# An mLSTM-and-bilinear kernel: a block's result copies move to the tiles in which weights were put together

## The chip, the cores and the metric

The kernel runs on one core of a Trainium2 chip. The metric is the time of one execution on the device in microseconds (us). Five engines work side by side, each through its own list of instructions in a fixed order: TensorE (PE; its weight loads are shown as PEld), VectorE (DVE), ScalarE (ACT), GpSimd (POOL), and SyncE (SP), which here only issues DMAs. An instruction that waits holds up all that stand behind it on its engine.

## The reference

Two stages follow each other. The first is an mLSTM attention over 4 batches, 8 heads, 768 steps and a head size of 40: a gated recurrence with a matrix state per head,

```
m_new = max(f + m, i);  F = exp(f + m - m_new);  I = exp(i - m_new)
C = F * C + I * v k^T;  n = F * n + I * k
y = sigmoid(o) * (C q) / max(|n.q|, 1)
```

The second takes y as 3072 tokens of 320 values and computes a bilinear feed-forward layer of width 1536:

```
a = x @ w_a;  b = x @ w_b;  out = (a * b) @ w_out
```

The three weight matrices arrive as 64-bit floats.

## The kernel before, in words

**Attention.** The tokens are cut into 24 chunks of 128 (6 time steps of a chunk for each of 4 batches). A chunk goes through a row of stages: its q and k are split into bf16 pieces and transposed by DMA, scores are made on PE (`pS`, line 468), weighted with exponentials of gate sums (ACT, line 413) and split again on DVE and ACT (lines 473 to 479, `pb`), multiplied with v (`pV`, line 520), joined with the state's share (`num`), divided and gated (`den`, `osig`, lines 591 to 613), and transposed on PE into x (`pX`, line 630). Output gates for four chunks are loaded and put through a sigmoid at once (`load_o`, line 169).

**Feed-forward.** Chunks form 9 blocks of 2 or 3 chunks: 2, 2, 3, 3, 3, 3, 3, 2, 3. `moe_block(kb)` walks through the width in 12 pieces of 128, `ff` = 0 to 11. `up(ff)` makes two products `acc[0]` and `acc[1]` of eight matmuls each (line 743) in PSUM, in three buffers that go round (tag `pu`). Line 750 copies `acc[0]` into a tile `g` in SBUF; DVE does it for ff = 1 and 2, ACT for all others. Line 751 (DVE) multiplies `acc[1]` into `g`. Lines 753 and 755 split `g` into `gh` and `gl`. `down(ff)` (line 716) follows two pieces later and adds to one PSUM tile `pd` for each chunk of the block. After ff = 11 each `pd` is copied by ACT to a tile `o` (line 725), and SP issues its DMA to `out` (line 726).

**Buffers.** `g` and `o` share a tag, `acp`, with three buffers of 384 fp32 values in each partition; a buffer comes free when the last reader of its tile is done, which for an `o` is its DMA. The tag `cv` has four buffers of the same size. They hold `cw`, in which a stage of the weights is put together from the halves of its 64-bit words (lines 342 to 375). The trace has the last instruction that touches a `cw` (line 373) at 92.3 us.

**Order.** While block kb runs through the feed-forward, the attention of a later block's chunks is handed out in between (`run_block`). For blocks 2 to 8 the order on PE and on SP is as the code is written; on ACT, DVE and POOL a planner sets it from its own estimate of when each instruction can start. SP takes its list in order: behind a block's last attention product it loads gate sums (`gbc`, line 180) and states (`cx`, line 587), and then come the `o` DMAs.

## Time and profile before

| | |
|---|---|
| median of 3 runs | 588.99 us (588.3 to 591.35) |
| the profiled execution, its own time | 591.32 us |
| its span, first to last instruction | 589.5 us |
| PE busy | 546.1 us (93%) |
| PEld busy | 516.2 us (88%) |
| DVE busy | 408.6 us (69%) |
| ACT busy | 221.8 us (38%) |
| POOL busy | 125.0 us (21%) |
| mean granted clock of TensorE | 0.948 |

A timeline row reads: start and length in us, engine, line, operation, what it writes and reads, how many were merged, and in brackets how long its engine stood idle before it and what ended that. A row of a view of waits reads: who waited for whom, us in total, how often, the longest. A row of the view by stretches gives, after the stretch and its length, the busy time of PE, PEld, DVE, ACT and POOL, each with its count of instructions, then the granted TensorE clock, the share of the DMA engines that was busy and GB/s.

### The profile page before, as it was taken

How to read it: one execution, taken by the hardware profiler on the slowest of the kernel's cores; microseconds unless marked ns; L12 is line 12 of the kernel's file. 1: busy time of each engine (PE TensorE's matmuls, PEld its weight loads, DVE VectorE, ACT ScalarE, POOL GpSimd, SP SyncE). 2: the span in 40 equal slices, each digit the busy share in tenths (PEclk: the TensorE clock that was granted, in tenths of full speed). 3: DMA queues.
4: the chain of work that ended last, by engine and by line, in shares of the span. 5: the costliest groups of instructions: out<-in, count | busy, mean ns of one | idle time of the engine just before them, and what ended most of it. 6: DMA issues, size and time to landing. Idle time of an engine off the chain costs nothing.

```text
span 589.5 us, 12444 instructions
## 1 busy us (share of the span) xinstructions
PE 546.1 (93%) x4810; PEld 516.2 (88%) x4810; DVE 408.6 (69%) x967; ACT 221.8 (38%) x530; POOL 125.0 (21%) x185
## 2 busy tenths in 40 slices
PE   9586899998999998999989998999969997899997
PEld 6485899987999987999879997999969997889997
DVE  6899676459978774878677893877649575744432
ACT  5677754434433451333431341542322324211011
POOL 2011245343332213033032132033020102000000
PEclk9687589989999999999989999899979999999999
DMA  9999513668838856358656665767543942300000
GB/s 182 277 271 271 104 37 83 130 102 146 163 92 167 145 99 131 70 113 174 102 122 132 102 123 129 101 134 154 79 110 40 166 75 71 73 1 24 0 1 34
DMA packets 198679, 66.77 MB, mean 113 GB/s; under 512 B 184252, under 2 KB 191900, under 8 KB 198620
## 3 DMA queue, kind: packets, MB, share of 16 engines
q1 hardware_dynamic: 198620, 65.98, 55.2%
q8 instruction: 38, 0.62, 0.5%
q14 instruction: 21, 0.17, 0.1%
HBM read 41.11 MB, written 5.97 MB: 80 GB/s over the span
## 4 chain that ended last, share of the span: by engine, by line
PE 69%; DMA 7%; DVE 4%; ACT 3%; issue 3%; SPq 2%; POOL 1%; POOLq 0%; ACTq 0%; DVEq 0%
PE pu L743 39%; PE pd L716 18%; PE pV L520 3%; DMA out_dram<-o 3%; PE pS L468 2%; PE pU L544 1%; DMA osig<-in_o_gate_dram 1%; PE pX L630 1%; SPq L587 1%; PE pI L494 1%; PE pS L817 1%; DMA T<-qks 1%; PE pV L869 1%; ACT gbc L413 1%; SPq L160 1%
## 5 line engine op out<-in xcount | busy, mean ns | idle before, releaser
L743 PE MATMUL pu<-xh,w 128*128 128x384 f32 (+1 forms) x1080 | 288.4, 334 | 20.6 <-ACT g L750 17.5
L743 PEld LDWEIGHTS pu<-xh,w 128*128 128x128 f32 x1080 | 198.6, 197 | 25.2 <-ACT g L750 19.4
L743 PE MATMUL pu<-xl,w 128*128 128x384 f32 (+1 forms) x648 | 214.2, 333 | 1.0 <-DVE xl L636 1.0
L716 PE MATMUL pd<-w,gh 128*128 128x320 f32 x576 | 133.4, 316 | 1.0 <-ACT gh L753 1.0
L743 PEld LDWEIGHTS pu<-xl,w 128*128 128x128 f32 x648 | 127.5, 197 | 2.0 <-DVE xl L636 1.3
L716 PEld LDWEIGHTS pd<-w,gh 128*128 128x128 f32 x576 | 98.4, 191 | 1.7 <-ACT gh L753 1.2
L751 DVE TENSOR_TENSOR g<-pu,g 128x384 f32<-128x384 f32 (+1 forms) x108 | 54.8, 507 | 58.7 <-PE pu L743 56.0
L750 ACT COPY g<-pu 128x384 f32<-128x384 f32 (+1 forms) x92 | 40.5, 441 | 139.6 <-PE pu L743 116.5
L716 PE MATMUL pd<-w,gl 128*128 128x320 f32 x288 | 89.9, 318 | 0.0
L455 POOL TENSOR_TENSOR vr<-va 128x336 f32<-128x336 f32 x18 | 13.6, 753 | 203.2 <-PE pV L520 188.0
L716 PEld LDWEIGHTS pd<-w,gl 128*128 128x128 f32 x288 | 54.3, 191 | 0.1
L413 ACT ACTIVATE gbc<-gbc,gtab 128x128 f32<-128x128 f32 x160 | 49.2, 390 | 11.6 <-POOL gbc L406 11.5
L755 DVE TENSOR_TENSOR gl<-g,gh 128x384 fp32r<-128x384 f32 (+1 forms) x92 | 50.3, 548 | 1.6
L527 DVE TENSOR_TENSOR num<-pV,num 128x336 f32<-128x336 f32 x18 | 9.1, 506 | 38.9 <-PE pV L520 38.8
L753 DVE CAST gh<-g 128x384 fp32r<-128x384 f32 (+1 forms) x96 | 34.0, 355 | 1.6
L475 ACT CAST pb<-gbc 128x512 bf16<-128x512 f32 x36 | 22.2, 617 | 20.4 <-DVE gbc L473 20.2
L562 ACT CAST cb<-cst 128x168 bf16<-128x168 f32 x18 | 6.0, 332 | 62.4 <-DMA gbc<-g_dram 40.8
L473 DVE TENSOR_TENSOR gbc<-pS,gbc 128x512 f32<-128x512 f32 x36 | 24.6, 683 | 5.2 <-PE pS L468 5.1
L406 POOL TENSOR_SCALAR_AFFINE_SELECT gbc<-gbc 128x1024 f32<-128x1024 f32 x20 | 23.4, 1168 | 21.6 <-DMA gbc<-g_dram 19.0
L520 PEld LDWEIGHTS <-pb 128*128 128x128 bf16 x576 | 23.1, 96 | 4.2 <-DVE pb L479 1.8
L520 PE MATMUL pV<-va,pb 128*128 128x42 bf16 x288 | 25.1, 182 | 1.6 <-DVE pb L479 1.6
L607 POOL TENSOR_TENSOR osig<-osig,den 128x320 f32<-128x320 f32 x22 | 16.9, 766 | 43.8 <-DVE den L602 25.4
(130 smaller groups left out, 804.0 us busy)
## 6 DMA issues: line engine op xcount, KB each, us to landing
gbc<-g_dram SPq DMA_DIRECT2D x20, 512.0 KB
qk<-in_q_dram SPq DMA_DIRECT2D x24, 160.0 KB
qk<-in_k_dram SPq DMA_DIRECT2D x24, 160.0 KB
va<-in_v_dram SPq DMA_DIRECT2D x24, 160.0 KB
osig<-in_o_gate_dram SPq DMA_DIRECT2D x24, 160.0 KB
raw<-in_moe_w_out_dram SPq DMA_DIRECT2D x12, 320.0 KB
out_dram<-o SPq DMA_DIRECT2D x24, 160.0 KB
raw<-in_moe_w_a_dram SPq DMA_DIRECT2D x8, 384.0 KB
```

The lines of the kernel that those rows point to most:

```text
L406: nc.gpsimd.affine_select(E, E, pattern=[[0, H], [1, P]], compare_op=ALU.is_ge, fill=-1e30, base=0, channel_multiplier=-1,)
L413: nc.scalar.activation(E[:, h], E[:, h], AF.Exp, bias=beta[:, h:h + 1])
L473: nc.vector.tensor_tensor(E, pS, E, op=ALU.mult)
L475: nc.scalar.copy(pb[:, 0], E)
L520: nc.tensor.matmul(pv[:, h], pb[i][:, h % HH, :], vb[j][:, h], start=(x == 0), stop=(x == len(terms) - 1),)
L607: (nc.vector if n < NS else nc.gpsimd).tensor_tensor(yv, yv, den.unsqueeze(2).broadcast_to([P, H, D]), op=ALU.mult)
L716: nc.tensor.matmul(pd[t][:, 0:DM], a[:, cols], w, start=(ff == 0 and first), stop=(ff == NF - 1 and last),)
L743: up_in = nc.tensor.matmul(acc[j], a, r, start=(x == 0), stop=(x == len(terms) - 1),).ins
L750: (nc.vector.tensor_copy if kb > 0 and ff in [1, 2] else nc.scalar.copy)(g, acc[0])
L751: nc.vector.tensor_tensor(g, acc[1], g, op=ALU.mult)
L753: (nc.vector.tensor_copy if kb > 0 else nc.scalar.copy)(gh, g)
L755: (nc.gpsimd if kb * 12 + ff < 16 else nc.vector).tensor_tensor(gl, g, gh.bitcast(F32), op=ALU.subtract)
```

## The change

Result tiles `o` of blocks 1 to 8 are taken from the four `cv` buffers instead of the three `acp` buffers. Block 0, during which weights are still put together, keeps `acp`. Sizes, instructions and DMAs are the same; no pool grows.

```diff
             if ff == NF - 1:
                 for t in range(sizes[kb]):
                     c, b = chunks[begins[kb] + t]
-                    o = mpool.tile([P, NTB], F32, tag="acp", name=f"o{kb}_{t}")[:, 0:DM]
+                    pool, tag, bufs = (cpool, "cv", CVB) if kb > 0 else (mpool, "acp", 3)
+                    o = pool.tile([P, WCH], F32, tag=tag, name=f"o{kb}_{t}", bufs=bufs)[:, 0:DM]
                     nc.scalar.copy(o, pd[t][:, 0:DM])
                     nc.sync.dma_start(out[b * S + c * P:b * S + (c + 1) * P, :], o)
```

The diff adds one line, so all below line 724 stands one line further down in the changed kernel (750 becomes 751). The orders of PE, SP and POOL are the same in both kernels. On ACT and DVE the planner places instructions differently around the ends of blocks. At the end of block 2 and the start of block 3 ACT's list reads, before (semaphores that an instruction waits for are in brackets; those of DMAs begin with DMAHW):

```order
L725 COPY o_0_3131<-pd_0_2187 128x320 [waits PE_49]
L725 COPY o_1_3134<-pd_1_2188 128x320 [waits DVE_49,PE_49]
L725 COPY o_2_3137<-pd_2_2189 128x320 [waits DVE_49,PE_49]
L562 CAST cb_3262<-cst_95 128x168 [waits DMAHW1_49,DMAHW0_49,DMAHW6_49,DVE_49,DMAHW7_49,Activation_49,Pool_49]
L750 COPY g_0_3157<-pu_0_0_3143 128x384 [waits DMAHW1_49,PE_49,Activation_49]
```

and in the changed kernel:

```order
L726 COPY o_0_3131<-pd_0_2187 128x320 [waits PE_49]
L726 COPY o_1_3134<-pd_1_2188 128x320 [waits PE_49]
L726 COPY o_2_3137<-pd_2_2189 128x320 [waits PE_49]
L751 COPY g_0_3157<-pu_0_0_3143 128x384 [waits DVE_49,PE_49]
L562 CAST cb_3262<-cst_95 128x168 [waits DMAHW1_49,DMAHW0_49,DMAHW6_49,DVE_49,DMAHW7_49,Activation_49,Pool_49]
```

The first copy of the next block's `g` no longer waits for a DMA, and it stands ahead of a state's cast (`cb`). The starts of blocks 4, 5, 6 and 7 lose the same wait.

On DVE, from the same place on, before:

```order
L527 TENSOR_TENSOR num_3018<-pV_3167,num_3018 128x336
L600 SCALAR_TENSOR_TENSOR den_3234<-num_3018 128x8
L601 TENSOR_SCALAR den_3234<-den_3234 128x8
L602 RECIPROCAL den_3234<-den_3234 128x8
L555 TENSOR_TENSOR cst_95<-pU_3241,cst_95 128x168
L610 TENSOR_TENSOR osig_2498<-num_3018,osig_2498 128x320
L435 TENSOR_TENSOR r_0_3307<-qk_80,qks_89 128x320
L612 COPY osig_2498<-osig_2498 128x64
L436 CAST qks_89<-r_0_3307 128x8x40
L750 COPY g_1_3253<-pu_1_0_3227 128x384
L751 TENSOR_TENSOR g_0_3157<-pu_0_1_3144,g_0_3157 128x384
```

and in the changed kernel:

```order
L527 TENSOR_TENSOR num_3018<-pV_3167,num_3018 128x336
L600 SCALAR_TENSOR_TENSOR den_3234<-num_3018 128x8
L752 TENSOR_TENSOR g_0_3157<-pu_0_1_3144,g_0_3157 128x384
L601 TENSOR_SCALAR den_3234<-den_3234 128x8
L754 CAST gh_0_3223<-g_0_3157 128x384
L602 RECIPROCAL den_3234<-den_3234 128x8
L756 TENSOR_TENSOR gl_0_3225<-g_0_3157,gh_0_3223 128x384
L555 TENSOR_TENSOR cst_95<-pU_3241,cst_95 128x168
L610 TENSOR_TENSOR osig_2498<-num_3018,osig_2498 128x320
L751 COPY g_1_3253<-pu_1_0_3227 128x384
```

The three steps on `g` of ff = 0 now stand between the attention's steps, ahead of `g` of ff = 1. At the start of block 5, where a group of output gates is awaited, DVE's list in the changed kernel holds (`pb` of chunk 17, `osig` of chunk 16):

```order
L754 CAST gh_2_5230<-g_2_5209 128x384
L442 COPY qks_91<-qks_91 128x8x40
L610 TENSOR_TENSOR osig_5048<-num_4918,osig_5048 128x320
L477 TENSOR_TENSOR gbc_4659<-gbc_4659,pb_1_5257 128x512
L442 COPY qks_92<-qks_92 128x8x40
L756 TENSOR_TENSOR gl_2_5232<-g_2_5209,gh_2_5230 128x384
L612 COPY osig_5048<-osig_5048 128x64
```

Before, five instructions stood there between line 610 and line 612 (line 479 of the first half and line 442 twice among them); now there are three, and line 479 is ahead of line 610.

## The prediction

> **What bounds the kernel now.** I read the page first, for the engine that sets the pace and the costliest idle time in front of it.

> ```profile
> span 589.5 us, 12444 instructions
> L743 PE MATMUL pu<-xh,w 128*128 128x384 f32 (+1 forms) x1080 | 288.4, 334 | 20.6 <-ACT g L750 17.5
> ```

> By the table above PE is the busiest engine by far. In front of line 743, its main work, it stood idle for 20.6 us, and 17.5 us of that ended when ACT had copied a `g`. The view of waits tells what ACT waited for:

> ```profile
> PE pu L743 <- ACT g L750: 17.5, 7, 4.5
> ACT g L750 <- DMA out_dram<-o: 15.3, 5, 9.0
> DVE g L750 <- DMA out_dram<-o: 6.3, 4, 2.7
> ```

> Five of ACT's copies and four of DVE's waited for the landing of a result. The timeline around the start of block 3 shows one such place, for ACT, SP and PE in turn, and behind it the step of the chain of waits that holds the DMA:

> ```profile
> 225.20 1.31 ACT L725 COPY o<-pd 128x320 f32<-128x320 f32 x3 [3.98 <-PE pd L716]
> 234.73 0.48 ACT L750 COPY g<-pu 128x384 f32<-128x384 f32 x1 [1.86 <-DMA out_dram<-o]
> ...
> 230.71 1.40 SPq L726 DMA_DIRECT2D out_dram<-o  x3
> ...
> 235.26 0.69 PE L743 MATMUL pu<-xh,w 128*128 128x384 f32 x1 [2.88 <-ACT g L750]
> ```

> ```profile
> 230.71 3.92 DMA out_dram<-o
> 226.04 2.11 PE pu L743 x12
> ```

> ACT had the three `o` ready at 226.5 (225.20 + 1.31). Their DMAs stand on SP behind loads that wait for the attention, so they are issued only from 230.71 on and land 3.92 us later, at 234.63. The three `o` hold all three `acp` buffers, so `g` of ff = 0 starts only at 234.73, though its product was done by 228.15 at the latest (226.04 + 2.11 covers twelve matmuls, it needs eight). PE goes on into the third PSUM buffer and then stands for 2.88 us. The same rows for blocks 4 to 7:

> ```profile
> 302.30 0.45 PE L743 MATMUL pu<-xh,w 128*128 128x384 f32 x1 [2.44 <-ACT g L750]
> 368.13 0.67 PE L743 MATMUL pu<-xh,w 128*128 128x384 f32 x1 [2.58 <-ACT g L750]
> 435.00 0.69 PE L743 MATMUL pu<-xh,w 128*128 128x384 f32 x1 [4.51 <-ACT g L750]
> 496.10 0.38 PE L743 MATMUL pu<-xh,w 128*128 128x256 f32 x1 [3.03 <-ACT g L750]
> ```

> Together 2.88 + 2.44 + 2.58 + 4.51 + 3.03 = 15.44 us. Blocks 2 and 8 follow blocks with two chunks, whose two `o` leave a buffer free; no stall stands there.

> The stall also costs clock. Stretches behind the five stalls, and one from the undisturbed last block:

> ```profile
> 235.30:238.40 3.10, 3.10 (x10) 3.02 (x10) 2.68 (x8) 2.97 (x10) 0.70 (x2) 0.50 0.67 102
> 303.40:306.70 3.30, 3.30 (x17) 3.00 (x16) 3.07 (x9) 3.29 (x12) 0.53 (x1) 0.50 0.60 82
> 368.20:371.50 3.30, 3.30 (x11) 2.99 (x11) 2.31 (x7) 2.28 (x8) 0.82 (x2) 0.50 1.08 180
> 435.00:439.80 4.80, 4.80 (x27) 4.28 (x28) 2.89 (x7) 2.76 (x10) 0.00 (x0) 0.50 0.04 8
> 496.10:499.50 3.40, 3.40 (x32) 3.36 (x33) 3.17 (x9) 3.39 (x9) 0.21 (x1) 1.00 0.00 0
> 538.00:550.00 12.00, 12.00 (x73) 12.00 (x72) 5.92 (x12) 0.96 (x2) 0.00 (x0) 1.00 0.07 24
> ```

> At a granted clock of 0.50 PE made 10 matmuls in 3.10 us (0.31 us each), at 1.00 it made 73 in 12.00 us (0.16). Behind four of the five stalls it worked 3.10 + 3.30 + 3.30 + 4.80 = 14.50 us at half speed; at full speed that work takes 7.25 us, so 7.25 us were lost. Stalls and clock make 22.7 us.

> **The change part by part.** It adds no instruction and no byte, and SP's order stays, so the `o` still land at about the same distance behind their block.

> *What is removed.* `g` of ff = 0 in blocks 3 to 7 waits for its product and an old `acp` buffer only. At block 3 ACT is free at 226.5 and the product done by 228.15: the copy ends by 228.6 instead of 235.2, and PE, which needs that buffer 2.88 us before 235.26, that is at 232.4, doesn't stop. Gain over five blocks: 15.44 us, and 7.25 us of clock if nothing else stops PE there.

> *What is added: the `cv` buffers' own waits.* A block takes three of four, the next one those that the block before filled some 60 us earlier, and the weights have left them by 92.3 us, ahead of the first such `o` at 164.65:

> ```profile
> 164.65 0.87 ACT L725 COPY o<-pd 128x320 f32<-128x320 f32 x2 [4.56 <-PE pd L716]
> ```

> ```profile
> L373 DVE TENSOR_TENSOR w<-cw,w x36: 477/552/1096, 11.4 to 92.3; 128x384 fp32r<-128x384 f32 x16, 128x320 fp32r<-128x320 f32 x12, 64x384 fp32r<-64x384 f32 x8
> ```

> Cost 0.

> *What is moved on DVE.* Three steps on `g` of ff = 0 now stand ahead of the second copy. By the page they take 507, 355 and 548 ns, 1.41 us:

> ```profile
> L751 DVE TENSOR_TENSOR g<-pu,g 128x384 f32<-128x384 f32 (+1 forms) x108 | 54.8, 507 | 58.7 <-PE pu L743 56.0
> L753 DVE CAST gh<-g 128x384 fp32r<-128x384 f32 (+1 forms) x96 | 34.0, 355 | 1.6
> L755 DVE TENSOR_TENSOR gl<-g,gh 128x384 fp32r<-128x384 f32 (+1 forms) x92 | 50.3, 548 | 1.6
> ```

> Does DVE now hold PE? DVE's stretches from the attention's last product to PE's resumption are 229.40 to 235.26 and so on:

> ```profile
> 229.40:235.26 5.86, 2.98 (x29) 2.42 (x28) 3.13 (x10) 0.86 (x3) 4.30 (x6) 0.98 0.83 234
> ...
> sum 28.79, PE 13.35 PEld 11.11 DVE 14.75 ACT 4.12 POOL 18.58; mean PE 2.67 PEld 2.22 DVE 2.95 ACT 0.82 POOL 3.72
> ```

> At block 3 ten instructions with 3.13 us of work and the 1.41 us moved ahead let the second copy end at about 229.4 + 4.54 = 233.9. PE needs that buffer for the second product of ff = 2, three products behind 232.4 less the one matmul already done: about 23 matmuls of 0.16 us, at 236.1. So 2 us are left, and I cost the new order at nothing. If that cover were gone, DVE would set the pace and only its idle time in these stretches could be won: 28.79 - 14.75 = 14.0 us. The attention behind it has cover too: the next product with v stands at 251.53 and its last split ended at 248.61,

> ```profile
> 247.92 0.69 DVE L479 TENSOR_TENSOR pb<-gbc 128x512 bf16<-128x512 f32 x1
> 251.53 1.22 PE pV L520 x48
> ```

> 2.9 us of slack, with DVE itself moving up.

> *What is late next.* In block 5 a load of output gates stands on SP behind the `o` DMAs and doesn't move:

> ```profile
> 374.99 0.78 POOL L607 TENSOR_TENSOR osig<-osig,den 128x320 f32<-128x320 f32 x1 [4.53 <-ACT osig L167]
> ...
> 376.76 0.48 DVE L610 TENSOR_TENSOR osig<-num,osig 128x320 f32<-128x320 f32 x1
> ...
> 378.94 0.18 DVE L612 COPY osig<-osig 128x64 f32<-128x64 f32 x1
> ...
> 380.34 0.49 PE L630 MATMUL pX<-ident,osig 128*128 128x128 f32 x3
> ```

> POOL ends at 375.77, and that is when line 610 can start in the new order. Before, the seven instructions from line 610 to 612 took 376.76 to 379.12, 2.36 us; now there are five, 1.7 us by their share. So x is ready between 377.5 and 378.1. PE came there at 380.34 and now comes 2.58 + 1.65 = 4.2 us sooner, at 376.1; the third transpose, the one that reads line 612's result, follows some 0.3 us on. New wait: 1.1 to 1.7 us. I take 1.5, since the new five hold the longer kinds.

> Sum: 15.44 + 7.25 - 1.5 = 21.2 us. The profiled execution took 591.32 us, 2.3 us over the median; 591.32 - 21.2 = 570.1, and against the median of 588.99 **568** us.

> [...]

> **The rivals.**

> *DVE becomes the bound behind each boundary.* For it: DVE is busy for 2.68 of 3.10 us behind the stall of block 3. Against it: the 2 us above. Time: 588.99 - 14.0 = 575.0.

> *The half clock of three blocks has another cause and stays.* Then the stretches at 235, 303 and 368 remain slow wherever they fall, and only 4.80 / 2 = 2.40 us of clock is won: 15.44 + 2.40 - 1.5 = 16.3, 572.7 us. For it: a gap of 3.03 us cost no clock; against it: each slow stretch begins within 1.1 us of a resumption. [...]

> *Slower: the three steps of `g` hold up the attention's chain.* Place: DVE at the starts of blocks 3 to 7, where the denominator, the gate product and then x come 1.41 us later. If PE would then wait for x or for the product with v as long as it waited for the buffer, the stalls stay and 5 x 1.41 = 7.1 us come on top: 596. It decides once PE's slack behind line 479 is under 1.4 us plus what PE gains; the 2.9 us and DVE's 14 us of idle time speak against it.

> *The change doesn't do what it says.* Some other wait ends as late as the `o` at all five places: 589. ACT's idle time there names the DMA, the new list names none.

> *More is won,* since DVE's lighter backlog also shortens smaller waits inside blocks: 565.

> **How the numbers follow.** Chances: forecast 0.56, DVE 0.20, clock 0.08, slower 0.05, nothing 0.05, more 0.06. What a measurement of this kernel can tell from no change is about 0.5%, 2.9 us. Forecast, DVE, clock and more are faster (0.90), nothing is same (0.05), slower 0.05. The forecast's own range is 566.3 (all 22.7 us) to 571; the range goes up to DVE's 575 and 1.5 us past it, and down to near 565: 564.5 to 576.5.

> **What would show it.** No row in which a copy of line 750 (now 751) waits for `out_dram<-o`; the five rows of PE's waits gone; the granted clock 1.00 behind the starts of blocks 3 to 7; a wait of 1 to 2 us in front of line 630 in block 5; a span of about 568. Wrong would be: PE's idle time in front of line 743 again ended by `g` at the same places, with DVE (line 750 or 751) named; clock 0.50 without a stall; or PE idle in front of lines 520 and 630 by as much as it was before line 743.

## The result and the profile after

The changed kernel took 565.64 us (median of 4 runs, 564.22 to 567.64) against 590.17 us of the kernel before on the same chip (4 runs, 588.3 to 593.43): a ratio of 0.958, with a 95% interval of 0.952 to 0.964. The prediction was 568, with a range of 564.5 to 576.5.

The page of the changed kernel, whose profiled execution took 564.22 us: the span, the granted clock in 40 slices of the span, the two groups of the up-projection on TensorE (PE) and the copies of `g` on ScalarE (ACT). Line 743 has become 744, and 750 has become 751.

```profile
span 562.4 us, 12436 instructions
...
PEclk9587789999999999999999999999999999999999
...
L744 PE MATMUL pu<-xh,w 128*128 128x384 f32 (+1 forms) x1080 | 282.5, 328 | 3.9 <-DVE w L373 2.2
...
L751 ACT COPY g<-pu 128x384 f32<-128x384 f32 (+1 forms) x92 | 40.5, 440 | 114.4 <-PE pu L744 114.1
```

PE's idle time in front of its main work fell from 20.6 to 3.9 us, and `g` is no longer what ends most of it. Of ACT's 114.4 us of idle time ahead of its copies of `g`, 114.1 end when the product is ready: the DMA is gone from there. No slice behind the sixth shows a lowered clock.

The same place as in the prediction, the start of block 3 (its first product starts at 221.24 us now). First the changed kernel's timeline of ACT, then one row of SyncE (SP) from its full timeline, then what the view of the tile `o` says of who waits for it from 219 to 232 us.

```profile
220.56 1.31 ACT L726 COPY o<-pd 128x320 f32<-128x320 f32 x3 [3.98 <-PE pd L716]
222.86 0.48 ACT L751 COPY g<-pu 128x384 f32<-128x384 f32 x1 [0.99 <-PE pu L744]
227.90 0.33 ACT L562 CAST cb<-cst 128x168 bf16<-128x168 f32 x1 [4.57 <-DMA gbc<-g_dram]
```

```profile
226.07 1.40 SPq L727 DMA_DIRECT2D out_dram<-o  x3
```

```profile
who waited for it (us, times):
  POOL gbc L406: 0.2, 1
```

The stores are still issued late, at 226.07, 4.2 us after ACT had the last `o` (220.56 + 1.31 = 221.87). But the copy of `g` starts at 222.86, before they are even issued, and waits for nothing but its product. For the stores only POOL waits now, 0.2 us.

The view by stretches of the changed kernel, 15 us from the start of each of blocks 3 to 7 (columns as in the prediction):

```profile
221.24:236.24 15.00, 15.00 (x164) 14.13 (x163) 11.07 (x27) 5.22 (x15) 5.68 (x7) 1.00 0.48 120
284.07:299.07 15.00, 15.00 (x164) 14.13 (x163) 11.07 (x26) 6.39 (x16) 5.68 (x7) 1.00 0.52 121
345.46:360.46 15.00, 15.00 (x164) 14.13 (x163) 11.06 (x27) 6.23 (x15) 4.81 (x6) 1.00 0.78 153
408.18:423.18 15.00, 15.00 (x147) 14.45 (x146) 9.32 (x27) 5.49 (x16) 4.62 (x6) 1.00 0.46 118
464.69:479.69 15.00, 15.00 (x219) 14.73 (x218) 12.00 (x29) 6.49 (x16) 3.45 (x4) 1.00 0.59 124
```

PE is busy for all 15 us behind all five starts, at a granted clock of 1.00, and DVE has 3.0 to 5.7 us to spare in each.

Where the time went, by blocks. A block's time runs from its first up-projection product to that of the next; these are differences of two start times in the trace.

| us | before block 2 | 2 | 3 | 4 | 5 | 6 | 7 | 8 | sum 3 to 7 |
|---|---|---|---|---|---|---|---|---|---|
| before | 160.47 | 65.41 | 67.48 | 65.69 | 65.75 | 63.42 | 48.51 | 52.72 | 310.85 |
| after | 156.07 | 65.17 | 62.83 | 61.39 | 62.72 | 56.51 | 44.88 | 52.79 | 288.33 |
| difference | -4.40 | -0.24 | -4.65 | -4.30 | -3.03 | -6.91 | -3.63 | +0.07 | -22.52 |

Blocks 3 to 7 gave 22.5 us. The 4.4 us before block 2 can't be put down to the change: the first `o` that it moves, block 1's, is copied behind that point, and in the kernels of the experiments that do not work on the start, block 2 began anywhere from 156.4 to 160.7 us.

### The profile page after: what moved, and what is told of

The parts are those of the page before. It is cut to its first block, busy times and chain, and to the rows that moved or that the text cites. A ratio compares the mean times of both kernels' runs of the same rounds, so it can differ in the third digit from the quotient of the medians.

```text
span 562.4 us, 12436 instructions
## 1 busy us (share of the span) xinstructions
PE 534.6 (95%) x4810; PEld 505.9 (90%) x4810; DVE 411.9 (73%) x967; ACT 221.3 (39%) x530; POOL 126.6 (23%) x185
## 4 chain that ended last, share of the span: by engine, by line
PE 68%; DVE 5%; DMA 5%; issue 4%; ACT 3%; SPq 2%; POOL 1%; POOLq 0%; ACTq 0%; DVEq 0%
PE pu L744 39%; PE pd L716 18%; PE pV L520 3%; PE pS L468 2%; PE pU L544 2%; DMA osig<-in_o_gate_dram 1%; ACT gbc L413 1%; PE pX L630 1%; PE pS L818 1%; PE pI L494 1%; PE pV L870 1%; DMA T<-qks 1%; SPq L160 1%; DMA gbc<-g_dram 1%; DMA qk<-in_q_dram 1%
## 5 line engine op out<-in xcount | busy, mean ns | idle before, releaser
L744 PE MATMUL pu<-xh,w 128*128 128x384 f32 (+1 forms) x1080 | 282.5, 328 | 3.9 <-DVE w L373 2.2
L744 PE MATMUL pu<-xl,w 128*128 128x384 f32 (+1 forms) x648 | 210.7, 327 | 1.0 <-DVE xl L636 1.0
L744 PEld LDWEIGHTS pu<-xh,w 128*128 128x128 f32 x1080 | 194.1, 192 | 7.1 <-DVE w L373 3.4
L716 PE MATMUL pd<-w,gh 128*128 128x320 f32 x576 | 132.8, 315 | 1.0 <-ACT gh L754 1.0
L744 PEld LDWEIGHTS pu<-xl,w 128*128 128x128 f32 x648 | 124.7, 193 | 2.0 <-DVE xl L636 1.3
L716 PEld LDWEIGHTS pd<-w,gh 128*128 128x128 f32 x576 | 97.9, 190 | 1.6 <-ACT gh L754 1.2
L716 PE MATMUL pd<-w,gl 128*128 128x320 f32 x288 | 89.2, 315 | 0.0
L751 ACT COPY g<-pu 128x384 f32<-128x384 f32 (+1 forms) x92 | 40.5, 440 | 114.4 <-PE pu L744 114.1
L716 PEld LDWEIGHTS pd<-w,gl 128*128 128x128 f32 x288 | 53.8, 189 | 0.0
L756 DVE TENSOR_TENSOR gl<-g,gh 128x384 fp32r<-128x384 f32 (+1 forms) x92 | 50.3, 546 | 1.6
L754 DVE CAST gh<-g 128x384 fp32r<-128x384 f32 (+1 forms) x96 | 32.7, 341 | 1.6
L520 PEld LDWEIGHTS <-pb 128*128 128x128 bf16 x576 | 23.1, 96 | 4.2 <-DVE pb L479 1.8
L607 POOL TENSOR_TENSOR osig<-osig,den 128x320 f32<-128x320 f32 x22 | 17.0, 771 | 43.8 <-DVE den L602 25.4
L431 ACT CAST qks<-qk 128x320 bf16<-128x320 f32 x36 | 16.1, 452 | 27.3 <-DMA T<-qks 12.4
```

Of the source, the lines that this page charges most:

```text
L520: nc.tensor.matmul(pv[:, h], pb[i][:, h % HH, :], vb[j][:, h], start=(x == 0), stop=(x == len(terms) - 1),)
L607: (nc.vector if n < NS else nc.gpsimd).tensor_tensor(yv, yv, den.unsqueeze(2).broadcast_to([P, H, D]), op=ALU.mult)
L716: nc.tensor.matmul(pd[t][:, 0:DM], a[:, cols], w, start=(ff == 0 and first), stop=(ff == NF - 1 and last),)
L744: up_in = nc.tensor.matmul(acc[j], a, r, start=(x == 0), stop=(x == len(terms) - 1),).ins
L751: (nc.vector.tensor_copy if kb > 0 and ff in [1, 2] else nc.scalar.copy)(g, acc[0])
L754: (nc.vector.tensor_copy if kb > 0 else nc.scalar.copy)(gh, g)
```

## The experiments

My theory was that the `o` of a block hold all three buffers of the tag `acp` until their stores have landed, that ACT's first copy of `g` waits for that, and that PE's stall behind it also lowers the clock. The rivals were that the gain comes from the planner's new order on ACT and DVE, that three stores rather than one matter, and that the half clock has a cause of its own.

**The stores on another queue, buffers as before.**

```diff
-                    nc.sync.dma_start(out[b * S + c * P:b * S + (c + 1) * P, :], o)
+                    nc.scalar.dma_start(out[b * S + c * P:b * S + (c + 1) * P, :], o)
```

> The kernel before, with `o` still in the three `acp` buffers, but its DMAs issued by ACT right behind each copy instead of by SP. Theory (the stall is the time from the `o` copy to its landing, 9.4 us at block 3, of which 4.2 us is waiting in SP's list behind loads and 3.9 us the transfer): the first `o` lands some 4 us after its copy, about 229.7 where it was 234.6, before PE needs the buffer at 232.4; the five stalls go, the time from the first product of block 3 to that of block 8 falls from 310.85 us to 288 to 290, total about 567. Rival 1 (sharing the tag is the cause whatever the landing): 310, total 590. Rival 2 (the loads behind the `o` on SP are the cause, since they come 1.4 us sooner): 1.4 us for each of five blocks, 304.

Measured: 567.06 us (4 runs, 566.61 to 568.37), ratio 0.959 (0.954 to 0.965); blocks 3 to 7 in 287.90 us. The granted clock was 0.961 over the profiled run, where the kernel before had 0.945 on the same chip. ACT's timeline of this kernel at the start of block 3 (ACTq is ACT issuing DMAs):

```profile
225.29 0.82 ACTq L726 DMA_DIRECT2D out_dram<-o  x2
226.22 0.42 ACT L725 COPY o<-pd 128x320 f32<-128x320 f32 x1 [0.55 <-ACT o L725]
226.67 0.34 ACTq L726 DMA_DIRECT2D out_dram<-o  x1
227.19 0.48 ACT L750 COPY g<-pu 128x384 f32<-128x384 f32 x1 [0.55 <-DMA out_dram<-o]
232.06 0.33 ACT L562 CAST cb<-cst 128x168 bf16<-128x168 f32 x1 [4.39 <-POOL osig L607]
```

The copy of `g` still waits for a store, but for 0.55 us. The first store is issued at 225.29 instead of 230.71 us, as soon as its copy is done, and its buffer is free by 227.19. So of the wait before, the time on SP's list (5.1 us from the end of the first copy, 225.63, to 230.71) was the larger part and the landing (3.92 us) the smaller. The landing, too, is shorter than I expected: at most 1.9 us instead of some 4. By the view by stretches the DMA engines were busy for 0.48 of that time (225.29 to 227.19) and for 1.00 of it before (230.71 to 234.63); whether that is the reason was not tested. Both ways, a free buffer or an earlier store, win the same within 0.5 us over these blocks. In ACT's list `g` stands ahead of the state's cast (line 562) here as in the changed kernel, so this run does not test the rival of the planner's order.

**Both at once.** The changed kernel with the stores issued by ACT too.

```diff
-                    nc.sync.dma_start(out[b * S + c * P:b * S + (c + 1) * P, :], o)
+                    nc.scalar.dma_start(out[b * S + c * P:b * S + (c + 1) * P, :], o)
```

> The changed kernel, with the `o` DMAs issued by ACT. Theory (no one waits for the `o` any more, so their landing does not matter): blocks 3 to 7 take 288.3 us within 1; the output gates of block 5 are loaded 1.4 us sooner, so PE's wait of 0.8 us in front of line 630 there goes. Rival (ACT's issues hold up the `g` copies behind them): 1 us more in each block, 293.

Measured: 567.88 us (4 runs, 565.88 to 570.52), ratio 0.961 (0.955 to 0.967); blocks 3 to 7 in 288.12 us. There is nothing left for the second remedy to take. The wait for x in block 5 did not go away as I expected: 0.68 us remained. Counted from the block's start (346.97 us), POOL's step on the gates (line 607) was done after 15.57 us instead of 16.52 in the changed kernel, but DVE came to line 610 only after 16.85 instead of 16.55, since until then it worked on other steps without a break. The last rows of its timeline up to there:

```profile
363.40 0.35 DVE L754 CAST gh<-g 128x384 fp32r<-128x384 f32 x1
363.67 0.23 DVE L442 COPY qks<-qks 128x320 bf16<-128x320 bf16 x1
363.82 0.48 DVE L610 TENSOR_TENSOR osig<-num,osig 128x320 f32<-128x320 f32 x1
```

So DVE's list bounds this x nearly as closely as the gates do.

**Block 5's copies alone** (they end block 5 and so act on the start of block 6).

```diff
-                    pool, tag, bufs = (cpool, "cv", CVB) if kb > 0 else (mpool, "acp", 3)
+                    pool, tag, bufs = (cpool, "cv", CVB) if kb == 5 else (mpool, "acp", 3)
```

> The change for the results of block 5 alone; all others stay in `acp`. Theory (each stall is its own and is won whole): block 6 takes 56.5 us instead of 63.4, with clock 1.00 at its start; blocks 3, 4, 5 and 7 stay at 67.5, 65.7, 65.8 and 48.5 within 0.3. Rival (a block that ends sooner only waits later): block 7 takes back more than 1 us.

Measured: 580.97 us in one run, blocks 3 to 7 in 67.41, 65.83, 65.76, 56.51 and 48.06 us. Block 6 alone went to its 56.51. Blocks 3, 4 and 5 stayed within 0.2 us of the kernel before; block 7 came out 0.45 us shorter, a little outside the 0.3 that I expected. The gain is local: each block's copies act on the start of the next block.

**The first copy alone in `cv`.** Of a block's three `o` the second and third stay in `acp`.

```diff
-                    pool, tag, bufs = (cpool, "cv", CVB) if kb > 0 else (mpool, "acp", 3)
+                    pool, tag, bufs = (cpool, "cv", CVB) if kb > 0 and t == 0 else (mpool, "acp", 3)
```

> The changed kernel, but only the first result copy of a block lies in a cv buffer, the second and third in acp. My theory: the stall needs all three acp buffers held by results, so one buffer free is enough for the first copy of g: blocks 3 to 7 take about 288.5 us (288.3 in the changed kernel), no TensorE idle time over 2 us at their starts. Rival: the copies of g of the next pieces wait for the second and third store as well, since these land only some 4 us later; then about half of the gain goes, about 300 us for blocks 3 to 7.

Measured: 564.61 us in one run, blocks 3 to 7 in 288.33 us. That this is the changed kernel's sum to the hundredth is chance, since single blocks differ by up to 0.15 us. One free buffer is enough.

**The stalls filled.** The kernel before, with throwaway matmuls between the two products of ff = 1, where PE stood; nothing reads what they write.

```diff
+                if j == 0 and ff == 1:
+                    for _ in range([0, 0, 0, 15, 13, 14, 24, 18, 0][kb]):
+                        nc.tensor.matmul(pd[0][:, 0:DM], xh[:, 0, 0:P], w_down(0)[0], start=True, stop=True)
```

> The kernel before, with extra matmuls on PE where it stands at the starts of blocks 3 to 7 (15, 13, 14, 24 and 18 of 128x320, about 0.15 us each, into a PSUM tile that the block clears later; they compute nothing that is used). The waits for the `o` stay, PE is busy in them. Theory (the half clock follows from the stall, 7.25 us in all): clock 1.00 at the starts of blocks 3 to 6, these four shorter by 1.5, 1.6, 1.6 and 2.4 us, blocks 3 to 7 together 303.6 us instead of 310.85. Rival (the half clock has another cause): the 0.50 stays and the blocks take 310 to 311. Rival (the extra work costs as much as the clock gives): over 311.

Measured: 582.2 us (4 runs, 581.74 to 582.55), ratio 0.985 (0.980 to 0.990). Blocks 3 to 7 took 304.59 us, 6.26 less than before. The granted clock was 0.971 over the profiled run (0.945 in that of the kernel before on the same chip), and no slice behind the tenth shows a lowered one. The granted clock in 40 slices of the span, from the pages of the kernel before and of this one (block 2 starts in the eleventh slice; before, block 3's half clock falls into two slices and does not show):

```profile
PEclk9687589989999999999989999899979999999999
...
PEclk9697689998999999999999999999999999999999
```

Work that computes nothing made the kernel 1.5% faster. So the half clock follows from the stall, and it is some 6 of the 22.5 us; the rest is the wait itself. I had expected 7.25. In block 6, for one, PE's timeline of this kernel has the fill from 423.05 us on and then 1.32 us of idle time, 4.99 us to the next product, where the stall had been 4.51:

```profile
423.05 3.67 PE L750 MATMUL pd<-w,xh 128*128 128x320 f32 x24
428.04 0.44 PE L743 MATMUL pu<-xh,w 128*128 128x384 f32 x1 [1.32 <-ACT g L753]
```

(`g` stands on line 753 here.) So `g` came somewhat later there, and the fill gave back some of the clock it kept.

```profile
231.65:235.06 3.41, 0.73 (x14) 0.42 (x9) 1.91 (x5) 0.66 (x2) 1.96 (x4) 1.00 0.97 272
235.06:238.47 3.41, 3.21 (x10) 3.06 (x10) 2.89 (x8) 3.21 (x11) 0.94 (x2) 0.50 0.71 111
491.06:494.47 3.41, 2.01 (x21) 1.76 (x19) 2.41 (x8) 0.62 (x1) 1.98 (x3) 1.00 0.76 188
494.47:497.89 3.42, 1.79 (x16) 1.75 (x17) 2.27 (x6) 2.19 (x4) 1.09 (x1) 1.00 0.30 110
497.89:501.30 3.41, 3.41 (x45) 3.31 (x43) 2.94 (x9) 2.43 (x8) 0.00 (x0) 1.00 0.02 5
```

Block 3's stall lies in one window almost whole: PE is busy there for 0.73 of 3.41 us, and the next window runs at 0.50. Block 7's stall, though longer, is cut by a border into two windows with 2.01 and 1.79 us of work, and both are followed by 1.00. That gave a theory to test: the share of work in a window sets the clock of the next. First the kernel before once more, in case the border lay elsewhere:

> The kernel before once more, as it stands, for a second profile with the clock's windows lying elsewhere. Theory of fixed windows: the granted clock changes only on a grid of 3.413 us, and a window in which TensorE stands idle for 1.97 us or more is followed by one at 0.50, one with 1.70 us or less by one at 1.00, whichever block it is. So each of the five stalls (2.4 to 4.5 us) costs clock if and only if one window holds more than about 1.8 us of it; the stall of block 7 may cost clock this time, and one of blocks 3 to 5 may keep it. Rival: the length of the gap or the block decides: 2.4 to 2.9 us in blocks 3 to 5 and 4.5 in block 6 lose the clock again, and block 7 (products of 256 columns) keeps it again.

Measured: 591.36 us in one run. The border fell in nearly the same places, so the same four stalls lost the clock and block 7's (2.90 us, cut into 1.28 and 1.62) kept it. The windows around the stalls agreed with the theory's numbers, but nothing told it from its rival. So I moved block 7's stall, with six throwaway matmuls in the block ahead of it:

```diff
+                if kb == 6 and ff == 1 and j == 1:
+                    for _ in range(6):
+                        nc.tensor.matmul(pd[0][:, 0:DM], xh[:, 0, 0:P], w_down(0)[0], start=True, stop=True)
```

> The kernel before with six throwaway matmuls of 320 columns behind the second product of ff = 1 of block 6 (nothing reads their results); they only move what follows by some 1.7 us. In two profiles of the kernel before, the stall of block 7 (3.03 and 2.90 us) was cut by a border of the clock's grid into 1.4 + 1.6 and 1.3 + 1.6 us, and kept the clock. Theory of fixed windows: moved by 1.7 us, most of the stall lies in one window, over 1.97 us, and the clock is 0.50 for 3.4 us behind it; block 7 takes about 50 us instead of 48. If the grid lies so that it is cut evenly again, it keeps the clock. Rival: block 7 keeps the clock because of what runs there (products of 256 columns); 1.00 behind the stall wherever the border lies.

Measured: the stall of 3.05 us now lies inside one window, and the next runs at half clock. Block 7 took 49.92 us instead of 48.51. By windows, from this kernel's trace:

```profile
490.72:494.14 3.42, 0.37 (x3) 0.17 (x3) 2.09 (x5) 1.16 (x3) 1.29 (x2) 1.00 0.77 236
494.14:497.55 3.41, 3.41 (x20) 3.32 (x21) 2.06 (x6) 3.40 (x9) 0.10 (x1) 0.50 0.00 0
497.55:500.96 3.41, 3.41 (x42) 3.31 (x41) 3.11 (x8) 0.78 (x2) 0.00 (x0) 1.00 0.02 5
```

In this kernel it was the place of the border, then, and not the block. The last question was what counts as work:

```diff
+                if j == 0 and ff == 1:
+                    for _ in range([0, 0, 0, 20, 16, 17, 30, 20, 0][kb]):
+                        nc.tensor.matmul(pd[0][:, 0:42], xh[:, 0, 0:P], w_down(0)[0][:, 0:42], start=True, stop=True)
```

> The kernel before, with the stalls at the starts of blocks 3 to 7 filled by throwaway matmuls of 42 columns (20, 16, 17, 30 and 20 of them, nothing reads their results), so that the profile shows TensorE busy while it moves few columns. Theory that the clock follows the columns moved and not the busy time of the profile: the clock is 0.50 for 3.4 us behind most of the stalls all the same, blocks 3 to 7 take about 309 to 311 us. Rival, any matmul keeps the clock: 1.00 behind all five, as with the fill by matmuls of 320 columns, 304 to 305 us.

Measured: 590.79 us in one run, blocks 3 to 7 in 311.74 us, nothing won over the kernel before (310.85). The clock was 0.50 for one window behind the fill of block 3 and for two behind those of blocks 5 and 6; it stayed at 1.00 in block 4, where a border cut the fill, and in block 7, where 1.23 us of the window went to other products (0.76 us in block 5's, beside sixteen more narrow ones). Block 5, first the fill in the timeline of PE, then two windows:

```profile
362.22 1.97 PE L750 MATMUL pd<-w,xh 128*128 128x42 f32 x17
```

```profile
360.86:364.27 3.41, 3.33 (x38) 2.92 (x36) 1.47 (x3) 0.33 (x1) 1.44 (x3) 1.00 0.99 317
364.27:367.68 3.41, 2.51 (x8) 2.51 (x9) 2.60 (x7) 2.83 (x9) 1.60 (x3) 0.50 1.01 184
```

The profile shows PE busy for 3.33 of 3.41 us, and the clock dropped all the same, to 0.50. Seventeen matmuls of 42 columns took 1.97 us, 0.116 each, where 24 of 320 columns took 3.67 in the fill before, 0.153 each. So the busy time of the profile did not tell that this window would lose the clock. Behind the fill of 24 wide matmuls in block 6 the page shows no lowered clock; behind seventeen narrow ones here it was 0.50.

**Earlier output gates.** In the changed kernel PE still waits for x in block 5. The view of the tile `osig` there, from 355 to 364 us, three of its rows (start times are the last numbers ahead of the shape), and PE's row of the timeline:

```profile
L167 ACT ACTIVATE osig<-osig x1: 1277/1277/1277, 359.9 to 359.9; 128x1280 f32<-128x1280 f32 x1
L607 POOL TENSOR_TENSOR osig<-osig,den x1: 727/727/727, 361.2 to 361.2; 128x320 f32<-128x320 f32 x1
...
L612 DVE COPY osig<-osig x1: 185/185/185, 363.6 to 363.6; 128x64 f32<-128x64 f32 x1
```

```profile
363.88 0.33 PE L630 MATMUL pX<-ident,osig 128*128 128x128 f32 x1 [0.83 <-DVE osig L612]
```

The sigmoid of four chunks' gates ends at 361.2, and the chain over lines 607, 610 and 612 to PE hangs on it. A chunk's steps are handed out by a pattern, a string with one letter for each slot. For every fourth chunk (those that load gates) I used a second pattern, in which `O`, the load of the gates, comes ahead of `G` and `C`, the loads of gate sums and states. One slot of `d`, the transposes for the chunk before, moves ahead with it:

```diff
     PATTERN = "LbababPaBaBaBaiaaGvdvdCedOeeececfufuu"
+    PATTERN_O = "LbababPaBaBaBaiaadOGvvdCedeeececfufuu"
...
-        for o in PATTERN:
+        for o in (PATTERN_O if n % B == 0 else PATTERN):
```

> The changed kernel, and in every fourth chunk, in which a group of output gates is loaded, that load is issued some slots earlier. If the new wait that the change left at the start of block 5 (0.83 us in front of the transposes of x) and its like at 276.73 us (0.68) come from the late output gates, both go, and blocks 3 to 7 take about 286.8 instead of 288.3 us. Rival: the x of these chunks is bound by the steps on VectorE and not by the gates; then the waits stay at 0.7 to 0.8 us and the sum at 288.3.

Measured: 562.68 us (6 runs, 560.68 to 563.92), ratio 0.954 (0.950 to 0.957) to the kernel before; blocks 3 to 7 in 285.48 us, 2.85 less than in the changed kernel and nearly twice the 1.5 us that I expected. Block 2 gained as well (63.61 instead of 65.17 us). Block 5's rows from its timeline:

```profile
349.74 1.28 ACT L167 ACTIVATE osig<-osig 128x1280 f32<-128x1280 f32 x1
352.61 0.93 POOL L607 TENSOR_TENSOR osig<-osig,den 128x320 f32<-128x320 f32 x1 [0.92 <-issue]
...
355.89 0.49 DVE L612 COPY osig<-osig 128x64 f32<-128x64 f32 x1
363.46 0.49 PE L630 MATMUL pX<-ident,osig 128*128 128x128 f32 x3
```

x is ready 7 us before PE comes for it. PE no longer has a gap over 0.6 us from the start of block 2 to 481 us, and blocks 3, 4 and 5 take 61.39, 61.39 and 61.36 us. The gates came some 11 us earlier, counted from the block's start, and DVE's steps on them moved up by some 9 us. So the run shows that the waits go when gates and steps move up together; with gates that came only 1 us sooner, in the run with both remedies, 0.68 us remained.

**Throwaway work at the start.** Between the first product of block 0 and that of block 2 the changed kernel ran 27.9 us at half clock. I put throwaway matmuls into PE's gaps there (nothing reads them).

```diff
+    def fill(t, n):
+        for _ in range(n):
+            nc.tensor.matmul(t[:, 0:NTB], w_up(0, 0, 0)[0], ws[0][:, 0], start=True, stop=True)
...
+        if n == 0:
+            fill(pU, 16)
...
+        if n == 1:
+            fill(pX, 9)
...
+            if n == 2 and j == 0:
+                fill(pT, 9)
```

> The changed kernel with 34 throwaway matmuls of 128x384 in the idle time of TensorE before block 2 (nothing reads what they write). In the changed kernel TensorE works 27.9 us at half clock there. If that half clock comes from the idle gaps as it did behind the five stalls, filling them takes it away, and the time falls by up to half of it, 14 us; as the start also waits for weights I expect 3 to 10 us (555 to 562). Rival: the start is bound by loads and by VectorE, not by TensorE's clock: within 2 us of 565.6, whatever the clock does.

Measured: three runs from 563.05 to 564.77 us, above the 555 to 562 that I expected and 1 to 3 us below the rival's 565.6; a fourth took 1276.41 us at a granted clock of 1.00, which nothing here explains, and is left out of the comparison (ratio 0.956, 0.951 to 0.960). Block 2 began at 151.35 us instead of 156.07, with 17.5 us at half clock in that stretch. But block 7 took 2.6 us more than in the changed kernel: its scores waited 2.12 us for a transpose by DMA, and the window that held this gap was followed by one at half clock (granted clock 0.976 over the profiled run). That wait is 0.56 us in the changed kernel's profile, and under 0.6 in that of the last kernel below, so it moves from run to run and this run alone does not say what the fill is worth.

**Both additions.**

> Both edits at once, earlier output gates and throwaway matmuls before block 2, on top of the changed kernel. If the two gains are at different places they add up: what each brought alone, 1.5 + 3 to 10 us, so 554 to 561 us. Rival: neither place bounds the end, 564 to 567 us.

Measured: 557.85 us (5 runs, 555.01 to 557.95), ratio 0.946 (0.941 to 0.950). The runs lie wholly below those of the earlier gates alone on the same chip (560.68 to 563.92). Two stretches of this kernel and the two that answer to them in the changed kernel, up to the start of block 2:

```profile
17.00:60.00 43.00, 33.18 (x204) 29.39 (x205) 35.96 (x78) 27.50 (x61) 6.62 (x10) 0.78 0.98 260
60.00:151.70 91.70, 89.93 (x840) 84.94 (x840) 73.70 (x175) 52.27 (x139) 39.59 (x53) 0.99 0.64 122
```

```profile
15.76:60.00 44.24, 33.16 (x218) 28.02 (x217) 40.58 (x90) 31.29 (x71) 5.16 (x11) 0.73 1.04 284
60.00:156.07 96.07, 89.72 (x798) 84.48 (x798) 70.69 (x164) 48.75 (x131) 39.34 (x53) 0.95 0.57 106
```

The second stretch holds 42 more matmuls in 4.4 us less, at a mean clock of 0.99 instead of 0.95. This version is faster than both kernels (its ratio to the kernel before, 0.941 to 0.950, lies below the changed kernel's 0.952 to 0.964); the part that the fill has in it is about 4.8 us by the two medians (562.68 - 557.85).

## Why the prediction was right

**The five stalls, 15.44 us:** right. They are gone in the changed kernel, and with the block 5 copies alone only block 6's went. The view of the waits named the store by itself; the run with the stores on ACT's queue showed that the order on SP is what made them late.

**The clock, 7.25 us:** right in kind. It is the one term with a rival that a run could price apart: filling the stalls won 6.26 us. The reason I could not give, why 3.03 us kept the clock, is the border of a window of 3.413 us. By the windows of the kernel before, the gaps of 2.44 to 2.88 us in blocks 3 to 5 each lay almost whole in one window, which had 2.39 to 2.68 us of idle time in its 3.41 and was followed by 0.50; block 7's 3.03 us were cut into windows with 1.41 and 1.62 us, both followed by 1.00. The rival of 572.7 us, another cause for the half clock of blocks 3 to 5, fell with the filled stalls, behind which the page shows no lowered clock.

**DVE at the new order, costed at nothing:** right. It was busy for 11.07 of 15.00 us behind the start of block 3 while PE never stopped; no wait of PE for a copy of DVE appeared. DVE's first copy of `g` at block 3 ended 8.1 us behind the block's start (229.35 - 221.24), where I had worked out 8.0 (233.9 - 225.88). The rival of 575.0, DVE as the bound, did not come, nor did the slower one: the attention's chain had its cover.

**The `cv` buffers, costed at nothing:** right; only POOL waits for a store, 0.2 us.

**The new wait in block 5, 1.5 us:** mis-sized; 0.83 us. The two ends that I worked out were 1.1 and 1.7. From the block's start at 345.46 the last of x is ready after 18.33 us (363.79; I had worked out 18.4 to 19.0 from 359.05), and PE comes for the third transpose after 17.59 (363.88 - 0.83; I had 17.35). Each end was off by 0.1 to 0.7 us, and both errors make the wait shorter. That line 610 starts when POOL is done was right for the changed kernel (16.55 us against 16.52), but the gates are only part of the cause: with gates 1 us earlier the wait stayed, since DVE came no sooner, and it went when the gates and DVE's steps moved up together.

**The sum, 21.2 us:** 22.52 in blocks 3 to 7. Of the 1.3 us that I missed, 0.3 are block 5 (3.03 against 2.58 + 1.65 - 1.5 = 2.73) and 0.6 block 7 (3.63 against 3.03), where a wait in front of the scores shrank from 0.80 to 0.56 us and the rest was not traced (the two profiles of the kernel before have 48.51 and 47.78 us for this block, so it varies by as much); blocks 3 and 4 have 0.2 each. The median is a further 1 to 2 us lower, which lies within what the start of this kernel varies by from run to run. So the rival "more is won", 565 us, is nearer to the measured 565.64 than the forecast, but not for the reason I gave: PE's smaller waits inside block 3 are 1.05 us where they were 1.12, and blocks 4 and 6 have none in either kernel beside the stall.

What stays open is the share of the planner's new order on ACT and DVE. The order and the free buffer were never run one without the other, since the planner sets the order from the waits; the run with the stores on ACT's queue has the new order at this place too. The order alone cannot do it: before, `g` began at 234.73 us, right behind the landing at 234.63 that freed its buffer, and SP's order is the same in both kernels. But the free buffer in the old order would not have won all either. ACT's row ahead of that `g`, before:

```profile
232.54 0.33 ACT L562 CAST cb<-cst 128x168 bf16<-128x168 f32 x1 [6.03 <-DMA gbc<-g_dram]
```

Behind this cast, which waits for a load, `g` (0.48 us) could have ended at 233.35 at the earliest, 0.97 us after PE needed it (232.38). An estimate from the same rows of the other blocks gives 0.97 us in blocks 4 and 5, 1.5 in block 7, where a split of `pb` stands ahead, and nothing in block 6. By this estimate some 4.4 of the 15.44 us of stalls hang on the new order as well as on the buffer, and the other 11 on the buffer alone. The prediction went by the new order in ACT's list and did not price this share.

## What to carry to other kernels

A copy for a store that shares its buffers with a working tile binds the work to the place of the store in its queue's list, not only to its flight time (at block 3, 5.1 us of list and 3.92 us to the landing): look for a compute instruction that waits for an `out` DMA, and give it one buffer from a tag that is idle by then, or issue the store from a queue where nothing waits ahead of it. Here one remedy was enough (blocks 3 to 7 in 288.33 us with the buffers alone, 287.90 with the queue alone, 288.12 with both), and so was one buffer (288.33); but see that the freed instruction does not stand behind another one that waits. When a stall on TensorE is priced, look at the granted clock behind it too: in the profile of the kernel before, the five windows behind 80 us with 1.97 us of idle time or more were each followed by 3.41 us at 0.50, which at full speed would have held the work in 1.7 us.

## What the runs showed of the hardware

**The clock's window.** From 80 us on, the profiles of the kernel before and of the changed one hold 289 windows of the grid (148 and 141). By PE's busy time in the trace, 282 of them were followed by a clock of 1.00, and none of these had more than 1.69 us of idle time in its 3.41 us (the changed kernel's from 124.99 us on). Seven were followed by 0.50, and six of these had 1.97 to 2.86 us. The seventh, from 119.01 us on in the kernel before, had 0.41 us; it holds sixteen matmuls of 40 rows and 42 columns each (at 120.40 us). In the run with the narrow fill, block 5's window with 0.08 us was followed by 0.50 as well. So in these profiles the idle time told the two kinds of window apart where matmuls are wide, and did not where they are narrow. Counting columns sorts these windows better. Take the columns that a matmul moves (384 in a product of line 743 over three chunks) and add them up over the matmuls that begin in a window. The seven windows that were followed by 0.50 have sums of 636 to 2976, the 282 others 3008 and more. In the run with the narrow fill, block 5's window, which lost the clock, has 2538, and block 7's, which kept it, 3144. But the sums of the two kinds overlap when more runs are taken: in the second run of the kernel before, the window from 95.84 to 99.26 us (eight matmuls of 40 rows and 42 columns, eight of 40 rows and 128 columns, and products of 256 columns) has at least 3152, and behind it such a product took 0.41 us instead of 0.28. What exactly the chip counts was not measured.

**A gap's length alone says little.** Gaps of 2.12 us (the start-up fill, block 7) and 2.44 us (block 4 before) cost clock, and gaps of 3.03 and 2.90 us (block 7 before) did not: the border cut these into 1.41 and 1.62 us and into 1.28 and 1.62.
